# Attention and an MLP mixer on one core: next batch's work shared out by phase, low parts one product later, weight sums moved to VectorE

## The chip, the cores and the metric

The kernel runs on one core of a Trainium2 chip. The time is the device time of one execution in microseconds (us); lower is better. A core has five engines that each take their instructions from a queue in a fixed order: PE (TensorE, matmuls and transposes), DVE (VectorE), ACT (ScalarE), POOL (GpSimd) and SP (SyncE, which here starts DMA transfers). An engine whose next instruction waits for another engine holds everything that is queued behind it.

## The reference

There are B=8 batches, H=8 heads, S=576 positions and D=64 dims per head, all in f32. Attention comes first: a downsampled one (means over 4 positions, 144 x 144 scores) and a local one (each position sees those less than 4 away), added. Then a token MLP and a channel MLP with residuals.

```python
q_d, k_d, v_d = means of q, k, v over 4 positions
out_up = repeat(softmax(scale * q_d @ k_d.T) @ v_d, 4)
out_local = softmax(where(abs(i - j) < 4, scale * q @ k.T, -1e9)) @ v
x = (out_up + out_local) laid out as [B, S, H*D]          # 576 x 512
h = relu(x.T @ w_tok1) @ w_tok2                           # 512 x 576, hidden 256
u = x + h.T
out = u + relu(u @ w_ch1) @ w_ch2                         # hidden 1536
```

## The kernel before, in words

**Numbers.** A product of f32 matrices is emulated: each operand is scaled by a power of two and parted into a high and a low f16 part, and `mm3` (L122 to L124) issues three matmuls, high x high and the two mixed ones. High parts are mostly written by ACT, low parts mostly by DVE, by a subtraction of the high part from the source.

**Stages.** For each batch there is attention, then the token MLP (`mix`, L661), then the channel MLP. Attention consists of four pieces of downsampled attention (two heads each, `pooled`) and five tiles of 128 rows (the last has 64) of local attention (`local`). A local tile goes through a chain of engines: scores `sc` (PE, L600), exponentials into `P` (ACT, L614), division by their sums (DVE, L619), transposes `pT` (PE, L623), their copy `pt` (ACT, L627), the product with the values `av` (PE, L636), and its copy `x` (ACT, L641). `mix` then makes f16 parts `xh` (ACT L678, DVE L680), the first token product `t1`, its ReLU `hid` (ACT L716, DVE L718), the second token product `t2`, and its eviction `u` (ACT L729) with a maximum `umx` (DVE L731). Of these maxima `everywhere` (L645 to L659) makes one scale: a transpose `um_t` and a small matmul `um_b` on PE with reductions on DVE between them. Last, `mixtures` (L761) cuts the operands of the first channel product: it forms sums and differences of quarters of `u` on POOL (L771) and parts seven blocks a11, s1, s2, a12, s4, s3 and a22 (ACT L782, DVE L784).

**Channel MLP.** For batches 0 and 1 the first product c1 is plain (`first`, `first_up`): 12 blocks of 128 hidden channels in each of two chunks of positions (256 and 320 wide), evicted by ACT (L876) and DVE (L878). From batch 2 on it is `product7` (L881): seven half-size products take the place of eight, for each of six pairs p of hidden blocks. They run in three PSUM banks P, Q and R; ACT copies partial results out (`plain`, L903: x1, m5 and u2), DVE adds the next product (x1 += Q L937, u2 += R L941, m5 += P L945), and `leave` (L906) makes of the four results the parts of `h`: the high part with the ReLU on ACT (L908), and at once the low part on DVE (L909). Each product is six matmuls. The seven products need three sums of weight blocks for each pair, `t123`, loaded by DMA (L918). The second product c2 (`second`, `second_up`) has four blocks of output rows in two chunks, 36 matmuls each, and DVE adds the result to `u` (L1021), which SP stores.

**Weight sums.** `weight_sums` (L963) makes these sums once, for six pairs. For each pair DVE adds high and low parts of four weight blocks back to f32 (L973: a1, b1, a2 and b2, in a pool "tm" of 6 buffers), POOL takes four differences (L983, L984, L988 and L993), and `parts` cuts each: the high part by ACT (L979), the low part by POOL (L980). Three results go to DRAM over SP (L990, L991), with two staging tiles ts12 and ts3 for all pairs; the fourth overwrites a part of the weights themselves (`CW`), so it has to follow the plain product of batch 1 that still reads them.

**Order.** The first part of the program, batch 0 and the preparation of weights, is ordered by a driver with due times (`drive`). From batch 1 on the channel MLP of batch b is the spine: after each of its steps `tick(n)` (L1125) emits steps of the side work, which is attention and `mix` of batch b+1 and the loads of batch b+2, until the side work that is emitted (in us of PE time by its own costs) has reached SIDE x done / (FR x 24 x S), with SIDE=42 and FR=0.9, where `done` counts the ticks. A batch has 24 x S ticks in all, half of them in the first product and half in the second. `weight_sums` takes turns with this side work from the second chunk of c1 of batch 1 on (L1141). Tile's scheduler then puts all that is emitted into one fixed order for each engine.

Of the kernel before, what the change touches and what calls it, by code (L numbers as in the profile page):

```python
# [14 lines left out]
ALU = mybir.AluOpType  # L15
# [28 lines left out]
def tile_ups_attention_mixer(ctx, tc, qk, vw, vr, w1, w2, c1, c2, out):  # L44
# [105 lines left out]
    def step(engine, us, *needs, at=None, take="", give=""):  # L150
        return engine, us, needs, at, take.split(), give.split()
# [729 lines left out]
    def product7(st, steps):  # L881
# [23 lines left out]

        def leave(src, r, i, h):  # L906
            o = h[:, i, :, HS * r:HS * r + HS]
            nc.scalar.activation(o[:, 0], src, AF.Relu)  # L908
            nc.vector.scalar_tensor_tensor(o[:, 1], src, 0.0, o[:, 0], ALU.max, ALU.subtract)  # L909
# [5 lines left out]
        for p in range(NP):  # L915
# [14 lines left out]
            m5 = plain(R, "m5", "A")  # L930
            yield step("P", us, ("uh", b, "s2"))
# [9 lines left out]
            nc.vector.tensor_tensor(u2, u2, R[:, :HS], ALU.add)  # L941
            leave(u2, 0, 1, h)
# [3 lines left out]
            leave(m5, 1, 1, h)  # L946
            if p + 1 < NP:
                yield step("P", us)
                old, P = P, bank(Qtag, "P")
                product(P, "a11", weights(fa + 2, 0), True, False)  # L950
                x1 = plain(P, "x1", "A")
            else:
                old = P
            yield step("P", us, ("uh", b, "a22"))
            product(old, "a22", weights(fb, 0), False, True)
            leave(old[:, :HS], 1, 0, h)
            for f in (fa, fb):
                make(("h", b, 0, f), now[0])
# [4 lines left out]
    def weight_sums():  # L963

        for p in range(NF // 2):
            sums.append(dram.tile([128, 3, 2, 256], F16, name=f"sums{p}"))
        for p in range(NF // 2):
            fa, fb = C1.fin[2 * p], C1.fin[2 * p + 1]
            y = {}
            for n, f, o in (("a1", fa, 0), ("b1", fb, 0), ("a2", fa, 256), ("b2", fb, 256)):  # L970
                yield step("V", 0.42)
                y[n] = T([128, 256], F32, "tm", f"{n}_{p}")
                nc.vector.tensor_tensor(y[n], f[:, 0, o:o + 256], f[:, 1, o:o + 256], ALU.add)  # L973
            if p == 0:
                ts12 = T([128, 2, 2, 256], F16, "uh", "ts12")
                ts3 = T([128, 2, 256], F16, "uh", "ts3")

            def parts(src, o):
                nc.scalar.copy(o[:, 0], src)  # L979
                nc.gpsimd.tensor_sub(o[:, 1], src, o[:, 0])  # L980

            yield step("G", 2.0)
            nc.gpsimd.tensor_sub(y["a1"], y["b1"], y["a1"])  # L983
            nc.gpsimd.tensor_sub(y["b1"], y["b2"], y["b1"])  # L984
            parts(y["a1"], ts12[:, 0])
            parts(y["b1"], ts3)
            yield step("G", 2.0)
            nc.gpsimd.tensor_sub(y["b2"], y["b2"], y["a1"])  # L988
            parts(y["b2"], ts12[:, 1])
            nc.sync.dma_start(sums[p][:, 0:2], ts12)  # L990
            nc.sync.dma_start(sums[p][:, 2], ts3)  # L991
            yield step("G", 2.0, ("c1", 1, 1, 2 * p + 1))
            nc.gpsimd.tensor_sub(y["a2"], y["a2"], y["b2"])  # L993
            parts(y["a2"], fb[:, :, 0:256])
        make(("sums",), now[0])
# [121 lines left out]
    for b in range(1, B):  # L1117
# [24 lines left out]
        else:  # L1142
# [3 lines left out]
            while g.next is not None:  # L1146
                g.go()
                tick(2 * S / 7)
        banks = {}
        g, u = Run(second(st, banks)), Run(second_up(st, banks))  # L1150
        for c in range(4):
            for ch in range(2):
                for k in range(3):
                    g.go()
                    if k == 2:
                        u.go()
                    tick(CHUNKS[ch][1])
# [50 lines left out]
```

## Time and profile before

| what | us |
|---|---|
| median of 3 runs | 987.17 |
| lowest and highest | 985.52 and 989.9 |
| the profiled execution | 980.41 |
| its span in the trace | 978.6 |
| mean granted TensorE clock | 0.967 |

The profile is of one execution, which took 980.41 us; its trace spans 978.6 us of that, and the remaining 1.8 us lie around the span. In the views below, "busy" counts the time in which an engine carries out instructions. PEclk is the granted TensorE clock as a share of full speed. A row of the timeline gives start, duration, engine, line, operation, result<-operands, size and, in brackets, how long the engine stood idle ahead of it and what released it. L numbers are lines of the kernel before.

### The profile page before, as it was taken

To read this page: it belongs to the slowest core of one execution; us is meant where nothing else is said; L and a number is where in the kernel's file an instruction comes from. 1 tells how busy PE (TensorE), PEld (TensorE's weight loads), DVE (VectorE), ACT (ScalarE), POOL (GpSimd) and SP (SyncE) were. 2 spreads that over 40 slices of the span, in tenths; PEclk is the share of its full clock that TensorE was granted. 3 is DMA by queue.
4 is the path that set the end of the run, shared out by engine and by line. 5 is a ranking of instruction groups with operands and counts; after the bars stand their busy time and mean duration, and the time that the engine had idled before them with its cause. 6 is when DMAs were issued, how large, how long until landed. Compare 5 with 4: busy or idle time off the path is not lost.

```text
span 978.6 us, 26351 instructions
## 1 busy us (share of the span) xinstructions
PE 898.3 (92%) x11218; PEld 662.2 (68%) x11218; DVE 530.0 (54%) x1263; ACT 426.2 (44%) x1028; POOL 305.8 (31%) x457
## 2 busy tenths in 40 slices
PE   7887899998879988899989999899989999899998
PEld 3544678677656756677766767577666767677786
DVE  7797886336572275624663266723764256723631
ACT  4764673335451165613662154712654145612520
POOL 5899940424763021602034021422034020002000
PEclk9778999999799989999999999999999999999999
DMA  9693331510325113510136013520136011100111
GB/s 260 181 300 103 117 85 37 176 45 29 96 61 164 35 40 105 185 36 25 55 98 178 19 37 99 160 61 25 52 84 195 25 36 42 46 28 25 56 30 37
DMA packets 35142, 84.87 MB, mean 87 GB/s; under 512 B 4272, under 2 KB 15536, under 8 KB 33776
## 3 DMA queue, kind: packets, MB, share of 16 engines
q1 hardware_dynamic: 32464, 80.82, 27.0%
q10 hardware_dynamic: 2560, 2.36, 0.9%
q8 instruction: 88, 1.44, 0.6%
q14 instruction: 30, 0.25, 0.1%
HBM read 69.01 MB, written 11.80 MB: 83 GB/s over the span
## 4 chain that ended last, share of the span: by engine, by line
PE 64%; DVE 15%; ACT 8%; POOL 6%; issue 4%; DMA 4%; ACTq 0%; POOLq 0%; SPq 0%; DVEq 0%
PE c L124 31%; PE t L124 9%; PE P L124 7%; PE ad L567 3%; PE R L124 3%; DMA vw<-od 3%; PE t L702 2%; ACT pd L551 2%; DVE xh L680 2%; PE td L558 2%; PE Q L124 1%; DVE h L909 1%; PE busy L168 1%; PE av L636 1%; PE sc L600 1%
## 5 line engine op out<-in xcount | busy, mean ns | idle before, releaser
L124 PE MATMUL c<-h,CX 128*128 128x320 f16 (+1 forms) x2304 | 304.2, 287 | 0.0
L124 PEld LDWEIGHTS <-CX 128*128 128x128 f16 x2304 | 223.3, 98 | 64.3 <-issue 3.4
L124 PEld LDWEIGHTS <-CW 128*128 128x128 f16 x1440 | 137.4, 100 | 46.0 <-issue 7.2
L487 POOL TENSOR_TENSOR vr<-vr 72x256 f32<-72x256 f32 x64 | 48.7, 760 | 194.1 <-ACT dump L484 193.7
L1021 DVE SCALAR_TENSOR_TENSOR u<-c,io,u 128x256 f32<-128x256 f32 (+1 forms) x64 | 33.0, 515 | 125.4 <-PE c L124 124.8
L771 POOL TENSOR_TENSOR s<-u,u 128x288 f32<-128x288 f32 x12 | 9.3, 796 | 266.9 <-ACT u L729 266.9
L729 ACT ACTIVATE u<-t,down 128x256 f32<-128x256 f32 (+1 forms) x64 | 29.9, 498 | 139.3 <-PE t L124 139.3
L124 PE MATMUL c<-uh,CW 128*128 128x256 f16 (+1 forms) x576 | 82.6, 296 | 0.2 <-DVE h L878 0.2
L124 PEld LDWEIGHTS <-t 128*128 128x128 f16 x648 | 61.5, 99 | 23.8 <-issue 8.3
L731 DVE TENSOR_REDUCE umx<-u 128x1 f32<-128x256 f32 (+1 forms) x64 | 27.8, 451 | 86.0 <-ACT u L729 86.0
L124 PE MATMUL t<-xh,W 128*128 128x512 f16 (+1 forms) x240 | 60.5, 385 | 4.1 <-DVE xh L680 3.6
L513 POOL TENSOR_TENSOR qs<-qk 128x288 f32<-128x288 f32 x56 | 42.5, 759 | 69.3 <-DMA qk<-in_qk_dram 65.3
L124 PE MATMUL t<-W,hid 128*128 128x256 f16 (+1 forms) x384 | 58.5, 289 | 0.0
L680 DVE SCALAR_TENSOR_TENSOR xh<-x,back,xh 128x512 f16<-128x512 f32 (+1 forms) x40 | 35.4, 886 | 28.8 <-ACT xh L678 28.8
L567 PE MATMUL ad<-vd,ptd 72*72 72x65 f32 x512 | 41.4, 236 | 5.5 <-issue 3.3
L678 ACT ACTIVATE xh<-x,back 128x512 f16<-128x512 f32 (+1 forms) x40 | 29.0, 726 | 39.5 <-PE t L124 37.3
L567 PEld LDWEIGHTS ad<-vd,ptd 72*72 72x72 f32 x512 | 38.5, 151 | 10.7 <-issue 4.9
L551 ACT ACTIVATE pd<-sd,nmd 72x144 f32<-72x144 f32 x128 | 37.5, 374 | 16.7 <-DVE nmd L546 13.0
L623 PE MATMUL pT<-ident,P 128*128 128x128 f32 (+1 forms) x160 | 25.7, 286 | 19.4 <-DVE P L619 12.6
L484 ACT ACTIVATE dump<-vr 72x512 uint8<-72x512 f32 x64 | 39.9, 624 | 7.5 <-DMA vr<-in_vr_dram 7.2
L641 ACT ACTIVATE x<-av,up 128x512 f32<-128x512 f32 (+1 forms) x40 | 27.2, 679 | 36.8 <-PE av L636 36.7
L716 ACT ACTIVATE hid<-t 128x512 f16<-128x512 f32 x16 | 9.6, 597 | 73.7 <-PE t L124 65.6
(182 smaller groups left out, 1635.6 us busy)
## 6 DMA issues: line engine op xcount, KB each, us to landing
qk<-in_qk_dram SPq DMA_DIRECT2D x32, 579.0 KB
t<-sums SPq DMA_DIRECT2D x36, 384.0 KB
vw<-in_vw_dram SPq DMA_DIRECT2D x32, 351.0 KB
vr<-in_vr_dram SPq DMA_DIRECT2D x64, 144.0 KB
C_raw<-in_c_dram SPq DMA_DIRECT2D x16, 512.0 KB
out_dram<-u SPq DMA_DIRECT2D x32, 160.0 KB
C_raws<-in_c_dram SPq DMA_DIRECT2D x8, 512.0 KB
out_dram<-u SPq DMA_DIRECT2D x32, 128.0 KB
```

The costliest lines, as they stand in the source:

```text
L124: nc.tensor.matmul(ps, lhs(a), rhs(c), start=first and i == 0, stop=last and i == 2, **kw)
L484: nc.scalar.activation(dump, t.rearrange("p r c -> p (r c)"), AF.Square, scale=2.0 ** -20, accum_out=st.vm[:, i:i + 1])
L487: nc.gpsimd.tensor_add(t[:, 0:2], t[:, 0:2], t[:, 2:4])
L513: nc.gpsimd.tensor_add(two, x[:, :, 0:2], x[:, :, 2:4])
L551: nc.scalar.activation(pd[:, par, g], s[:, par, g], AF.Exp, bias=nm[:, par, g:g + 1], scale=0.125 / 16)
L567: nc.tensor.matmul(ps[:, g, par], pt[:, par, kg, G * g:G * g + G], st.vd[:, kg, 2 * pr + par], start=kg == 0, stop=kg == 1)
L641: nc.scalar.activation(x.rearrange("p hp two d -> p two hp d"), ps[:n, :, :4 * D].rearrange("p two (hp d) -> p two hp d", hp=4), AF.Copy, ...
L678: nc.scalar.activation(st.xh[t][:, 0], xf(t), AF.Copy, scale=back[:n])
L680: nc.vector.scalar_tensor_tensor(st.xh[t][:, 1], xf(t), back[:n], st.xh[t][:, 0], ALU.mult, ALU.subtract)
L729: nc.scalar.activation(st.u[c][:, s0:s0 + N], banks[ch, c // 2][:, c % 2, :N], AF.Copy, scale=st.down)
L731: nc.vector.tensor_reduce(st.umx[:, ch, c:c + 1], st.u[c][:, s0:s0 + N], axis=AX.X, op=ALU.max, apply_absolute_value=True)
L1021: nc.vector.scalar_tensor_tensor(u, banks[c, ch], io[:, ch:ch + 1], u, ALU.mult, ALU.add)
```

## The change

It has three parts.

1. **Shares by phase.** In the loop around `product7` a tick counts two thirds of what it did, and in the loop around `second` four thirds for batches from 2 on. The total stays 24 x S, with 8 x S in the first product and 16 x S in the second. Batch 1 is not altered.
2. **Low parts later.** `leave` issues the high part and puts the low part on a list; `rests()` empties the list behind the next product's own eviction or addition. `leave(m5)` now stands behind the next pair's a11 product.
3. **Weight sums.** All four differences of a pair are taken by DVE, high parts are copied by POOL (a new instruction form there) in place of ACT, and low parts stay on POOL. Each difference and each parting is a step of its own, and each pair has a gate: it may start only when a named product of batch 1 has been emitted. Lines are shifted: in the kernel after, the sums are L984, the differences L991, the copies L993 and the low parts L994; `leave` is L910 and the low part L916.

```diff
+        later = []
         def leave(src, r, i, h):
             o = h[:, i, :, HS * r:HS * r + HS]
             nc.scalar.activation(o[:, 0], src, AF.Relu)
-            nc.vector.scalar_tensor_tensor(o[:, 1], src, 0.0, o[:, 0], ALU.max, ALU.subtract)
+            later.append((src, o))
+        def rests():
+            while later:
+                src, o = later.pop(0)
+                nc.vector.scalar_tensor_tensor(o[:, 1], src, 0.0, o[:, 0], ALU.max, ALU.subtract)
...
             m5 = plain(R, "m5", "A")
+            rests()
...
             nc.vector.tensor_tensor(u2, u2, R[:, :HS], ALU.add)
+            rests()
             leave(u2, 0, 1, h)
...
             nc.vector.tensor_tensor(m5, m5, P[:, :HS], ALU.add)
-            leave(m5, 1, 1, h)
+            rests()
...
                 product(P, "a11", weights(fa + 2, 0), True, False)
                 x1 = plain(P, "x1", "A")
+            leave(m5, 1, 1, h)
             yield step("P", us, ("uh", b, "a22"))
             product(old, "a22", weights(fb, 0), False, True)
+            rests()
             leave(old[:, :HS], 1, 0, h)
...
     def weight_sums():
+        gates = [("c1", 1, 1, 3), ("c1", 1, 1, 7), ("c1", 1, 1, 11), ("c2", 1, 0, 0), ("c2", 1, 1, 0), ("c2", 1, 0, 1)]
...
-                yield step("V", 0.42)
+                yield step("V", 0.42, gates[p])
                 y[n] = T([128, 256], F32, "tm", f"{n}_{p}")
                 nc.vector.tensor_tensor(y[n], f[:, 0, o:o + 256], f[:, 1, o:o + 256], ALU.add)
...
-            def parts(src, o):
-                nc.scalar.copy(o[:, 0], src)
-                nc.gpsimd.tensor_sub(o[:, 1], src, o[:, 0])
-            yield step("G", 2.0)
-            nc.gpsimd.tensor_sub(y["a1"], y["b1"], y["a1"])
-            nc.gpsimd.tensor_sub(y["b1"], y["b2"], y["b1"])
-            parts(y["a1"], ts12[:, 0])
-            parts(y["b1"], ts3)
...
+            for x, z, o in (("b1", "a1", ts12[:, 0]), ("b2", "b1", ts3), ("b2", "a1", ts12[:, 1]), ("a2", "b2", fb[:, :, 0:256])):
+                yield step("V", 0.42)
+                to = {("b1", "a1"): "a1", ("b2", "b1"): "b1", ("b2", "a1"): "b2", ("a2", "b2"): "a2"}[x, z]
+                nc.vector.tensor_tensor(y[to], y[x], y[z], ALU.subtract)
+                yield step("G", 1.5)
+                nc.gpsimd.tensor_copy(o[:, 0], y[to])
+                nc.gpsimd.tensor_sub(o[:, 1], y[to], o[:, 0])
...
-                tick(2 * S / 7)
+                tick(2 * S / 7 * 2 / 3)
...
-                    tick(CHUNKS[ch][1])
+                    tick(CHUNKS[ch][1] * (4 / 3 if b > 1 else 1))
```

Three places show how instructions move. The first is POOL while the weights are prepared, in batch 0. L231 and L234 cut weights of the second channel product (`C2_raw`); `a1_0` to `b2_0` are sums of pair 0, `a1_1` and `b1_1` of pair 1. Before:

```order
L231 TENSOR_SCALAR C2_raw3_1123<-C2_raw3_1123 128x512
L984 TENSOR_TENSOR b1_0_3520<-b2_0_3550,b1_0_3520 128x256
L988 TENSOR_TENSOR b2_0_3550<-b2_0_3550,a1_0_3517 128x256
L234 TENSOR_SCALAR C2_raw2_1113<-C2_raw2_1113 128x512
L231 TENSOR_SCALAR C2_raws4_1129<-C2_raws4_1129 128x512
L993 TENSOR_TENSOR a2_0_3524<-a2_0_3524,b2_0_3550 128x256
L983 TENSOR_TENSOR a1_1_3605<-b1_1_3625,a1_1_3605 128x256
L234 TENSOR_SCALAR C2_raw3_1123<-C2_raw3_1123 128x512
```

After, the same stretch of POOL holds the weight cutting alone; the five differences that stood here and a little ahead of it are on DVE.

The second place is DVE in the first product of batch 1, second chunk. `h1_0` is the output of the blocks `c1_1_1_0` and `c1_1_1_1`, `a1_3` to `b2_3` belong to pair 3 of the weight sums, and `ad2_2`, `rd2_2` and `od2` to the third downsampled piece of batch 2. Before:

```order
L878 SCALAR_TENSOR_TENSOR h1_0_3109<-c1_1_1_0_3491,h1_0_3109 128x320
L973 TENSOR_TENSOR a1_3_3907<-CW6_151 128x256
L973 TENSOR_TENSOR b1_3_3930<-CW7_152 128x256
L878 SCALAR_TENSOR_TENSOR h1_0_3109<-c1_1_1_1_3535,h1_0_3109 128x320
L973 TENSOR_TENSOR a2_3_3933<-CW6_151 128x256
L573 TENSOR_SCALAR rd2_2_3573<-ad2_2_3564 72x4
L574 RECIPROCAL rd2_2_3573<-rd2_2_3573 72x4
L575 TENSOR_TENSOR od2_3327<-ad2_2_3564,rd2_2_3573 72x4x64
```

After:

```order
L878 SCALAR_TENSOR_TENSOR h1_0_3109<-c1_1_1_0_3491,h1_0_3109 128x320
L984 TENSOR_TENSOR a1_3_4210<-CW6_151 128x256
L984 TENSOR_TENSOR b1_3_4229<-CW7_152 128x256
L984 TENSOR_TENSOR b2_3_4245<-CW7_152 128x256
L991 TENSOR_TENSOR a1_3_4210<-b1_3_4229,a1_3_4210 128x256
L991 TENSOR_TENSOR b1_3_4229<-b2_3_4245,b1_3_4229 128x256
L878 SCALAR_TENSOR_TENSOR h1_0_3109<-c1_1_1_1_3529,h1_0_3109 128x320
L573 TENSOR_SCALAR rd2_2_3557<-ad2_2_3548 72x4
L991 TENSOR_TENSOR b2_3_4245<-b2_3_4245,a1_3_4210 128x256
L574 RECIPROCAL rd2_2_3557<-rd2_2_3557 72x4
L984 TENSOR_TENSOR a2_3_4248<-CW6_151 128x256
L575 TENSOR_TENSOR od2_3327<-ad2_2_3548,rd2_2_3557 72x4x64
```

Between the eviction of block 0 and `od2` there were three sums and now stand four sums and three differences; the gates set when a step is emitted, and the scheduler's order of the engine puts it earlier than that.

The third place is ACT near the end of `product7` of batch 3, while the side work of batch 4 runs beside it. `h3_4` and `h3_5` are outputs of pairs 4 and 5; `pT4_1`/`pt4_1` and `av4_1`/`x4_1` belong to the second local tile of batch 4, `vr5` to values of batch 5, `xh4_0` to the token MLP of batch 4. Before:

```order
L627 COPY pt4_1_7030<-pT4_1_7025 128x512
L484 ACTIVATE dump_128,vm5_7444<-vr5_5_7626 72x512
L614 ACTIVATE P2_112<-P2_112 128x8x38
L484 ACTIVATE dump_128,vm5_7444<-vr5_6_7678 72x512
L908 ACTIVATE h3_4_7015<-x13_3_6962 128x288
L641 ACTIVATE x4_1_7121<-av4_1_7050,up4_6264 128x2x4x64
L908 ACTIVATE h3_4_7015<-u23_4_7037 128x288
L627 COPY pt4_2_7107<-pT4_2_7102 128x512
L678 ACTIVATE xh4_0_7340<-x4_1_7121,back_129 128x512
```

After, these rows stand where pair 5 ends and c2 of batch 3 begins:

```order
L910 ACTIVATE h3_5_6998<-m53_5_7006 128x288
L484 ACTIVATE dump_128,vm5_7523<-vr5_7_7768 72x512
L910 ACTIVATE h3_5_6998<-P_3_4_6941 128x288
L627 COPY pt4_1_7153<-pT4_1_7148 128x512
L614 ACTIVATE P2_112<-P2_112 128x8x38
L641 ACTIVATE x4_1_7235<-av4_1_7177,up4_6278 128x2x4x64
L627 COPY pt4_2_7215<-pT4_2_7210 128x512
L678 ACTIVATE xh4_0_7420<-x4_1_7235,back_129 128x512
L627 COPY pt4_3_7243<-pT4_3_7238 128x512
```

The copies of local tiles 1 to 3 stood among evictions of `product7`, from pair 4 on; now they follow the last eviction of pair 5. On PE, 12 matmuls of c2 stand between `pT4_1` and `av4_1`, and 12 more between `pT4_2` and `pT4_3`. The last `t2` product of a batch stood 72 matmuls of c2 ahead of the next `product7` and now stands 48 ahead.

More of the change, by code (lines that the diff above doesn't have):

```diff
@@ L945, in product7 @@
             nc.vector.tensor_tensor(m5, m5, P[:, :HS], ALU.add)
-            leave(m5, 1, 1, h)
+            rests()
+            old = P
             if p + 1 < NP:
                 yield step("P", us)
-                old, P = P, bank(Qtag, "P")
+                P = bank(Qtag, "P")
                 product(P, "a11", weights(fa + 2, 0), True, False)
                 x1 = plain(P, "x1", "A")
-            else:
-                old = P
+            leave(m5, 1, 1, h)
             yield step("P", us, ("uh", b, "a22"))
             product(old, "a22", weights(fb, 0), False, True)
+            rests()
             leave(old[:, :HS], 1, 0, h)
-            for f in (fa, fb):
-                make(("h", b, 0, f), now[0])
+            if p + 1 == NP:
+                rests()
         make(("h", b), now[0])
@@ L969, in weight_sums @@
             y = {}
-            for n, f, o in (("a1", fa, 0), ("b1", fb, 0), ("a2", fa, 256), ("b2", fb, 256)):
-                yield step("V", 0.42)
+            for n, f, o in (("a1", fa, 0), ("b1", fb, 0), ("b2", fb, 256), ("a2", fa, 256)):
+                yield step("V", 0.42, gates[p])
                 y[n] = T([128, 256], F32, "tm", f"{n}_{p}")
@@ L976, in weight_sums @@
                 ts3 = T([128, 2, 256], F16, "uh", "ts3")
-            def parts(src, o):
-                nc.scalar.copy(o[:, 0], src)
-                nc.gpsimd.tensor_sub(o[:, 1], src, o[:, 0])
-            yield step("G", 2.0)
-            nc.gpsimd.tensor_sub(y["a1"], y["b1"], y["a1"])
-            nc.gpsimd.tensor_sub(y["b1"], y["b2"], y["b1"])
-            parts(y["a1"], ts12[:, 0])
-            parts(y["b1"], ts3)
[L987 to L994, printed above, removed]
+            for x, z, o in (("b1", "a1", ts12[:, 0]), ("b2", "b1", ts3), ("b2", "a1", ts12[:, 1]), ("a2", "b2", fb[:, :, 0:256])):
[5 more added lines that the diff above has]
+                nc.gpsimd.tensor_sub(o[:, 1], y[to], o[:, 0])
+                if o is ts3:
+                    nc.sync.dma_start(sums[p][:, 2], ts3)
+                if to == "b2":
+                    nc.sync.dma_start(sums[p][:, 0:2], ts12)
         make(("sums",), now[0])
```

## The prediction

> **What bounds the kernel now.** I read the busy time by engine first.
>
> ```profile
> PE 898.3 (92%) x11218; PEld 662.2 (68%) x11218; DVE 530.0 (54%) x1263; ACT 426.2 (44%) x1028; POOL 305.8 (31%) x457
> ```
>
> PE is busy for 898.3 of 978.6 us. The change takes no work from PE, so all that it can win is in the 80.3 us in which PE stands idle, and in the time in which PE runs at a lower granted clock. Where these lie is shown by busy time in windows that I cut at the stage bounds. Columns: window, length, busy us (x instructions) of PE, PEld, DVE, ACT and POOL, then PEclk, DMA share and GB/s. The rows are c1 and c2 of batch 1, then `product7` and c2 by turns for batches 2 to 6, then `product7` of batch 7.
>
> ```profile
> 215.50:286.90 71.40, 59.32 (x824) 45.13 (x822) 43.90 (x104) 37.15 (x104) 42.85 (x64) 0.90 0.18 56
> 286.90:348.00 61.10, 58.96 (x614) 42.88 (x613) 19.78 (x47) 14.73 (x32) 18.87 (x34) 0.97 0.33 103
> 348.00:408.60 60.60, 52.95 (x952) 39.61 (x952) 43.49 (x106) 40.24 (x103) 14.29 (x23) 0.94 0.32 100
> 408.60:460.40 51.80, 51.80 (x394) 38.42 (x393) 14.29 (x39) 8.71 (x19) 13.39 (x24) 1.00 0.18 54
> 460.40:520.80 60.40, 52.87 (x980) 39.74 (x979) 43.65 (x107) 39.92 (x105) 14.30 (x23) 1.00 0.33 103
> 520.80:572.50 51.70, 51.70 (x393) 38.32 (x391) 14.20 (x38) 8.61 (x19) 13.29 (x24) 1.00 0.20 54
> 572.50:634.30 61.80, 54.10 (x984) 40.03 (x982) 44.99 (x108) 40.06 (x106) 14.96 (x25) 1.00 0.34 107
> 634.30:687.30 53.00, 51.55 (x395) 38.28 (x394) 15.33 (x39) 10.38 (x23) 13.89 (x23) 1.00 0.16 46
> 687.30:745.40 58.10, 53.33 (x969) 40.24 (x970) 41.31 (x104) 37.83 (x100) 12.42 (x21) 0.97 0.35 106
> 797.10:856.10 59.00, 52.98 (x980) 39.83 (x978) 42.03 (x106) 35.39 (x89) 1.51 (x2) 1.00 0.15 45
> 907.20:940.50 33.30, 32.17 (x261) 25.15 (x259) 18.99 (x46) 16.77 (x41) 0.00 (x0) 1.00 0.18 54
> ```
>
> Two kinds of stage lose time. The five `product7` stages with side work leave PE idle for 7.65, 7.53, 7.70, 4.77 and 6.02 us, 33.67 in sum, while the c2 stages between them leave at most 1.45, with DVE busy for 14 us of 52 and ACT for 9. The last `product7`, without side work, loses 1.13. And c1 of batch 1, in which the weight sums are made, leaves 12.08 us idle at a mean clock of 0.90.
>
> What PE waits for in one `product7` stage (460.4 to 520.8) is told by PE's waits. Columns: line, releaser, total us, count, longest.
>
> ```profile
> PE pT L623 <- DVE P L619: 2.5, 4, 1.2
> PE P L124 <- ACT x L903: 1.4, 2, 0.8
> PE av L636 <- DMA vw<-od: 1.0, 1, 1.0
> PE sc L600 <- ACT x L641: 0.8, 1, 0.8
> PE td L558 <- ACT pd L551: 0.6, 1, 0.6
> PE P L124 <- DVE x L937: 0.5, 1, 0.5
> ```
>
> The chains of attention own 2.5 + 0.8 + 0.6, the first products (P <- x) own 1.4 + 0.5, and one transfer owns 1.0: 6.8 of 7.53 us; smaller waits share the remaining 0.7.
>
> **The shares by phase.** Two thirds of the tick means that PE's order has about two products between pieces of attention where it had one and a half. A product lasts 32.17 / 42 = 0.77 us in the stage without side work, so a chain step gets 1.53 us of cover for 1.15. The longest wait on a chain step is 1.2 us, beyond the cover of 1.15; with 0.38 us more, waits under that size go and the larger ones shrink. What remains of the local tiles moves into c2, where by the order 12 matmuls stand between one step and the next.
>
> ```profile
> 457.19 3.43 PE L124 MATMUL c<-h,CX 128*128 128x320 f16 x24
> ```
>
> That is 1.72 us for 12, by the row of 24 matmuls of c2, and c2 has DVE and ACT nearly free. So of a stage's 7.53 us I let the attention waits go (7.53 less 1.9 for the first products and 1.0 for the transfer, which the change doesn't touch): -4.6. Taken back: c2 holds some chain waits that it didn't have, and only 12 matmuls in place of 24 stand between the last `t1` and the first `t2` while ACT and DVE make `hid`. I put 0.8 on that, between 0 (all covered by 1.72 us a step) and 2.5 (the four transposes wait as now).
>
> The scale of the mixtures comes out of `um_t` and `um_b`, and what then comes first in `product7` is the block a11. These are its rows on PE and on ACT.
>
> ```profile
> 457.94 0.96 ACT L782 ACTIVATE a11h<-u,us 128x288 f16<-128x288 f32 x2 [6.15 <-DVE us L130]
> 460.46 0.90 PE L124 MATMUL P<-a11h,CW 128*128 128x288 f16 x6
> 464.33 0.90 PE L124 MATMUL P<-s2h,t 128*128 128x288 f16 x6 [0.85 <-ACT x L903]
> ```
>
> ACT stood idle for 6.15 us until the scale came, and parted a11 at 457.94; PE had c2 matmuls to do until 460.46, so 1.6 us were to spare behind ACT's part. In the order, the last `t2` now stands 48 matmuls ahead of P instead of 72: 24 matmuls, 3.43 us, less. The distance from `um_b` to P shrinks only from 24 to 20 matmuls, 0.57 us of the 1.6. It still holds, but the mixtures on POOL and the parts on ACT start that much later, and `product7` takes up one block after another: I take +0.5 a batch (0 to 3.4, if all the lead was needed). Per batch this is -4.6 + 0.8 + 0.5 = -3.3, and for five batches **-16.5**, between about -30 (all idle time but the start's last microsecond goes) and +3.
>
> Batch 1's c2 isn't re-shared, but the order has the last `t2` of batch 2 behind its last matmul, where 12 matmuls followed before: **+1.7**, the cover that is gone.
>
> **Low parts later.** As many instructions as before. DVE's additions into x1, u2 and m5, on which a bank's release hangs, no longer queue behind a low part. P <- x L937 (0.5) may go; as more of `h`'s low parts end later, the last of them could meet c2's first matmuls, but c2 starts with pair 0. Counted at nothing, within -0.5 and +0.5 a batch.
>
> **Weight sums at the start.** In batch 0 five differences leave POOL, by the timeline:
>
> ```profile
> 72.81 1.17 POOL L983 TENSOR_TENSOR a<-b,a 128x256 f32<-128x256 f32 x1 [0.36 <-DVE b L973]
> 81.47 0.86 POOL L984 TENSOR_TENSOR b<-b,b 128x256 f32<-128x256 f32 x1
> 82.41 1.64 POOL L988 TENSOR_TENSOR b<-b,a 128x256 f32<-128x256 f32 x1
> 86.80 0.72 POOL L993 TENSOR_TENSOR a<-a,b 128x256 f32<-128x256 f32 x1
> 87.48 0.73 POOL L983 TENSOR_TENSOR a<-b,a 128x256 f32<-128x256 f32 x1
> 85.50 0.69 DVE L239 SCALAR_TENSOR_TENSOR CX<-C_raw 128x512 uint32<-128x512 uint32 x1 [1.25 <-POOL C_raw L234]
> ```
>
> They take 1.17 + 0.86 + 1.64 + 0.72 + 0.73 = 5.12 us of POOL, which cuts `C_raw` there while DVE waits for it (1.25 in the last row). DVE takes them into such waits. From 5.12 not all is on the path: **-2**, between 0 and -5.
>
> **Weight sums in c1 of batch 1.** This is what happens there now (timeline, then groups with count and busy, mean or shortest/mean/longest ns, and the windows around the stall):
>
> ```profile
> 251.52 0.88 DVE L973 TENSOR_TENSOR b<-CW 128x256 f32<-128x256 f16 x1 [1.93 <-POOL CW L980]
> 254.37 1.09 PE L623 MATMUL pT<-ident,P 128*128 128x128 f32 x4 [3.84 <-DVE od L575]
> 286.46 0.63 PE L623 MATMUL pT<-ident,P 128*128 128x128 f32 x4 [2.91 <-ACT ts L979]
> L973 DVE TENSOR_TENSOR a<-CW x12: 407/710/1296, 67.5 to 279.0; 128x256 f32<-128x256 f16 x12
> L980 POOL TENSOR_TENSOR ts<-b,ts x12: 661/672/903, 227.3 to 288.6; 128x256 f16<-128x256 f32 x12
> L979 ACT CAST ts<-b x12: 388/405/421, 225.1 to 286.0; 128x256 f16<-128x256 f32 x12
> L231 POOL TENSOR_SCALAR C_raw<-C_raw x16: 650/797/1690, 38.9 to 79.8; 128x512 uint32<-128x512 uint32 x16
> 222.00:225.50 3.50, 1.00 (x14) 0.52 (x10) 2.40 (x7) 3.08 (x10) 2.15 (x4) 1.00 0.01 2
> 225.50:230.00 4.50, 4.50 (x29) 3.44 (x30) 2.95 (x12) 2.64 (x9) 3.88 (x7) 0.62 0.17 62
> 254.40:264.00 9.60, 9.60 (x77) 6.53 (x78) 5.25 (x10) 3.53 (x10) 8.90 (x15) 0.51 0.20 72
> ```
>
> A sum on DVE waits for a buffer of "tm" that POOL still reads, `od` queues behind the sum, and PE waits for `od`: 3.84 us idle, and then 9.60 us at a clock of 0.51, which costs 9.60 x 0.49 = 4.7 more. One such jam is worth 8.5 us. The Trainium skill ("TensorE: Matmul & The Clock Gate", Part 1) says that the clock halves after an idle window of about 3.4 us and returns after about as long a busy one. By it a jam would cost 3.84 + 1.7 = 5.5; the row of 9.60 us at full busy time and 0.51 speaks against so quick a return, and 0.62 in the 4.50 us behind a window with 2.50 us of idle time against so long an onset, so I keep 4.7.
>
> What the change does: 24 casts leave ACT (24 x 0.405 = 9.7 us). 19 differences leave POOL, at 0.72 to 0.86 each 14 to 16 us, and come to DVE (19 x 0.41 to 0.71 = 8 to 13 us). 24 high parts come to POOL; a copy there isn't in the trace, so it lies between 0.33 (half of the shortest L231, which has twice the elements) and 0.67 (L980, of the same size with one operand more). I take 0.5, nearer to the row of one operand: 12 us, with 8 to 16 as ends. So POOL has 39 to 41 us, DVE 52 to 57, ACT 27: none reaches 71.4. It is a matter of order. DVE's queue now holds every sum and difference, and each sum waits for a buffer that POOL must release: what is queued behind is `od`, the eviction of c1's blocks (L878) and, behind these, PE. By the order `od2_2` stands behind 4 sums and 3 differences where it stood behind 3 sums, so I keep the jam of 8.5 at that place, and let the wait for `ts` on ACT (2.91) go, as that instruction no longer exists. Against it I set 1.9, one wait of DVE for POOL (the 1.93 above) that passes to PE: **-1**, between -12 (idle time and half clock go) and +17 (two jams more).
>
> **The sum.** -16.5 + 1.7 - 2 - 1 = -17.8. From the profiled 980.41 us that gives 962.6; the median of the runs shown is 6.8 above the profiled one, so from 987.17 the forecast is 969.4, **969**. From 982.2 to 992.1, within 0.5% of the median, is about what a measurement of this kernel can tell from no change.
>
> **Rivals.**
>
> *The waits move along.* The waits of the local tiles might sit in the chain and not in the cover: then c2 stalls for what `product7` no longer does. For: pT waits for DVE P in both cases by order. Against: DVE and ACT are busy for a quarter and less of c2. Time: the term of -4.6 a batch falls away with its 0.8, leaving +0.5 x 5 + 1.7 - 2 - 1 = +1.2: 988. No change.
>
> *DVE jams on POOL, slower.* In c1 of batch 1 each sum may stall DVE, and PE behind it, for long enough to halve the clock, at 8.5 us a jam. For: POOL was the releaser of DVE's waits (1.93), and all buffers now pass through DVE, POOL and DVE again. Against: POOL's sum of work falls. It ends above 992.1 if 23 us more are lost, that is with three more jams: -17.8 + 25.5 = +7.7, 995.
>
> *Nearly all idle time goes.* -30 in `product7`, the jam and its half clock gone (-8.5) with the 2.91, and -3 at the start, +1.7: -42.7, 944. For: chains with 1.53 us of cover against waits of at most 1.2. Against: the first products' waits are not touched.
>
> *Both at once are slower on SBUF.* DVE's sum and POOL's subtraction ran side by side around 251.5 and the sum took 0.88 where the shortest took 0.41. If all 19 differences and 18 sums in the stage take 0.47 more, DVE has 17 us more, about 70 of 71.4, and becomes the bound there; half of the 17 would land on PE: 969 + 8.5 = 978. The Trainium skill ("GPSIMD Engine Reference", Specifications) says that GpSimd shares its SBUF interfaces with VectorE and contends with instructions of two SBUF inputs, which these are; the longest sum of 1296 ns agrees.
>
> **How the numbers follow.** The forecast has 0.57 (its own range 957 to 979), the waits that move 0.14, the jams 0.09, the larger gain 0.12, the contention 0.08. Faster by over 0.5%: 0.57 + 0.12 + 0.08 = 0.77; within: 0.14; slower: 0.09. The range reaches down to 947, which leaves out some of the larger gain, and up to 988, which leaves out the jams.
>
> **What would show it.** Right: `product7` stages with side work under 57 us with less than 4 us of idle PE, c2 stages longer by the work moved and with under 2 us idle; c1 of batch 1 within 71 +/- 5 us, a stall before `pT` of batch 2 behind `od`; POOL copies of about 0.5 us. Wrong: idle time in c2 as large as what left `product7`; PE waiting for `um_b` or a11 at the start of `product7`; a clock near 0.5 for more than 10 us of c1 of batch 1.

## The result, and the profile after

| | us |
|---|---|
| after, median of 4 runs | 962.63 (962.29 to 963.37) |
| before, median of 4 runs beside them | 986.35 (983.91 to 989.9) |
| ratio, 95% interval | 0.9758 (0.9726 to 0.9789) |
| the profiled execution of after, its span | 963.37, 961.6 |

The change makes the kernel 23.7 us faster by medians; 969 was forecast, in a range of 947 to 988. The two profiled executions differ by less: 978.6 - 961.6 = 17.0 us of span. Both differences are taken up below. Two executions in the experiments, one of 1728.49 us and one of 1257.29 us, lie far outside the other runs of their kernels and are left out of every figure.

The windows of the kernel after, cut at its own stage bounds, have the same columns as before: c1 and c2 of batch 1, `product7` and c2 for batches 2 to 6, then the last `product7`.

```profile
214.90:286.70 71.80, 59.87 (x889) 46.05 (x887) 52.30 (x126) 32.38 (x86) 44.63 (x74) 0.90 0.20 62
286.70:347.00 60.30, 56.66 (x553) 41.55 (x549) 17.83 (x45) 12.50 (x27) 14.87 (x27) 0.99 0.32 97
347.00:398.40 51.40, 47.87 (x682) 36.10 (x682) 36.08 (x88) 33.24 (x87) 9.57 (x14) 0.91 0.25 73
398.40:455.90 57.50, 57.42 (x665) 42.21 (x664) 21.24 (x56) 16.16 (x32) 18.01 (x32) 1.00 0.30 89
455.90:506.30 50.40, 46.36 (x708) 35.73 (x706) 35.99 (x90) 33.49 (x91) 9.53 (x14) 1.00 0.27 78
506.30:564.00 57.70, 57.49 (x664) 42.13 (x663) 21.15 (x56) 16.09 (x32) 17.92 (x32) 1.00 0.31 88
564.00:614.60 50.60, 46.66 (x711) 36.04 (x710) 36.34 (x90) 33.77 (x92) 9.74 (x15) 1.00 0.27 80
614.60:675.20 60.60, 58.33 (x671) 42.31 (x669) 23.55 (x59) 17.75 (x37) 19.12 (x33) 1.00 0.30 82
675.20:725.30 50.10, 45.95 (x698) 35.32 (x699) 33.96 (x87) 31.51 (x88) 7.67 (x13) 1.00 0.27 79
725.30:782.80 57.50, 57.42 (x665) 42.20 (x663) 21.31 (x55) 15.99 (x32) 17.88 (x33) 1.00 0.31 88
782.80:832.00 49.20, 46.19 (x707) 35.70 (x706) 35.07 (x90) 29.27 (x77) 1.97 (x2) 1.00 0.20 59
832.00:889.60 57.60, 57.19 (x661) 41.88 (x660) 21.96 (x50) 17.67 (x35) 6.01 (x8) 1.00 0.06 20
889.60:923.40 33.80, 32.03 (x259) 25.05 (x258) 21.61 (x51) 18.59 (x46) 0.51 (x1) 1.00 0.18 53
```

Read it row against row. `product7` of batch 3 was 60.40 us with 7.53 idle and is 50.40 with 4.04; the c2 behind it was 51.70, full, and is 57.70 with 0.21 idle. So 10 us left the one and 6 came to the other: work moved, and about 3.5 us of waiting didn't move with it. The five `product7` stages have 3.53, 4.04, 3.94, 4.15 and 3.01 us of idle PE, 18.67 in sum where there were 33.67. DVE in these c2 stages goes from 14 to 16 us to 21 to 24 and is still far from full.

PE's waits in `product7` of batch 3 (455.9 to 506.3) are now these, all that the view lists. Columns: line, releaser, total us, count, longest.

```profile
PE P L124 <- DVE m L954: 1.7, 1, 1.7
PE P L124 <- ACT x L903: 0.8, 1, 0.8
PE td L558 <- ACT pd L551: 0.8, 1, 0.8
PE Q L124 <- DVE h L916: 0.7, 1, 0.7
```

The four waits of `pT` for DVE (2.5), that of `sc` (0.8) and that of the transfer (1.0) are gone from this stage; the products wait for their own evictions (m, x, h) more than before, 3.2 us where they waited 2.1.

In c1 of batch 1 the timeline of PE has both old stalls again, the second a little later, and no wait for ACT's casts at the end:

```profile
227.51 0.28 PE L652 MATMUL vm_t<-ident,vm_m 72*1 72x72 f32 x1 [4.84 <-DVE vm_m L649]
257.00 0.99 PE L623 MATMUL pT<-ident,P 128*128 128x128 f32 x4 [3.93 <-DVE od L575]
342.74 0.27 PE L652 MATMUL um_t<-ident,um_m 128*1 128x128 f32 x1 [0.65 <-DVE um_m L649]
344.90 0.38 PE L658 MATMUL um_b<-um_m,ones 1*128 1x1 f32 x2 [1.90 <-DVE um_m L655]
347.00 0.40 PE L124 MATMUL P<-a11h,CW 128*128 128x288 f16 x1 [1.10 <-ACT a11h L782]
```

The last three rows are the end of c2 of batch 1, where the order had put the last `t2` behind all matmuls of c2: 0.65 + 1.90 + 1.10 = 3.65 us, with nothing to cover them. The stage is 60.30 long nevertheless, 0.8 less than before.

### The profile page after: what moved, and what is told of

Same layout as the page of the kernel before. It is cut to its first block, busy times and chain, and to the rows that moved or that the text cites. A ratio compares the mean times of both kernels' runs of the same rounds, so it can differ in the third digit from the quotient of the medians.

```text
span 961.6 us, 26341 instructions
## 1 busy us (share of the span) xinstructions
PE 892.8 (93%) x11218; PEld 660.7 (69%) x11218; DVE 538.3 (56%) x1287; ACT 424.7 (44%) x1004; POOL 300.2 (31%) x457
## 4 chain that ended last, share of the span: by engine, by line
PE 73%; DVE 16%; ACT 5%; issue 3%; DMA 1%; POOL 1%; ACTq 0%; POOLq 0%; DVEq 0%; SPq 0%
PE c L124 32%; PE t L124 10%; PE P L124 9%; PE R L124 4%; PE av L636 3%; PE ad L567 3%; PE sc L600 2%; PE t L702 2%; PE Q L124 2%; PE busy L168 2%; PE pT L623 2%; PE td L558 2%; PE sd L539 1%; DVE CX L239 1%; DVE uh L757 1%
## 5 line engine op out<-in xcount | busy, mean ns | idle before, releaser
L124 PE MATMUL c<-h,CX 128*128 128x320 f16 (+1 forms) x2304 | 310.0, 286 | 3.0 <-DVE u L949 2.0
L487 POOL TENSOR_TENSOR vr<-vr 72x256 f32<-72x256 f32 x64 | 52.6, 821 | 196.2 <-ACT dump L484 189.5
L513 POOL TENSOR_TENSOR qs<-qk 128x288 f32<-128x288 f32 x56 | 39.3, 701 | 94.5 <-DMA qk<-in_qk_dram 90.9
L680 DVE SCALAR_TENSOR_TENSOR xh<-x,back,xh 128x512 f16<-128x512 f32 (+1 forms) x40 | 33.0, 825 | 57.3 <-ACT xh L678 56.2
L124 PEld LDWEIGHTS <-hid 128*128 128x128 f16 x384 | 34.9, 99 | 11.1 <-ACT hid L716 1.8
L636 PE MATMUL av<-vw,pt 47*32 47x64 f32 x2304 | 36.5, 234 | 5.4 <-DMA vw<-od 3.4
```

The costliest lines, as they stand in the source:

```text
L124: nc.tensor.matmul(ps, lhs(a), rhs(c), start=first and i == 0, stop=last and i == 2, **kw)
L487: nc.gpsimd.tensor_add(t[:, 0:2], t[:, 0:2], t[:, 2:4])
L513: nc.gpsimd.tensor_add(two, x[:, :, 0:2], x[:, :, 2:4])
L636: nc.tensor.matmul(ps[QB * j:QB * j + QB, par, D * hp:D * hp + D], pt[p, hp, QB * j:QB * j + QB], st.vw[h][p, g, D * hp:D * hp + D], start ...
L680: nc.vector.scalar_tensor_tensor(st.xh[t][:, 1], xf(t), back[:n], st.xh[t][:, 0], ALU.mult, ALU.subtract)
```

## The experiments

Times are ratios to the kernel before, run beside it on the same chip. Kernels are compared by stages as well, because one part varies from execution to execution: the start. The kernel before was run unchanged for a second profile.

> The kernel before, unchanged, for a second profile. All theories: ratio 1.0 within the spread of 0.6%. If this execution is slower than the 980.4 of the first profile, the stage in which it is longer tells what varies: by theory C c1 of batch 1 (the clock after the stall); otherwise the start, or the product7 stages alike.

Its median was 985.76 against 985.2, ratio 1.0012 (0.999 to 1.0034). Its windows are the start (to c1 of batch 1), c1 and c2 of batch 1, and the five pairs of `product7` and c2 as one:

```profile
0.00:220.60 220.60, 191.85 (x2425) 133.30 (x2432) 153.27 (x344) 115.49 (x250) 126.07 (x171) 0.90 0.47 143
220.60:352.80 132.20, 114.47 (x1437) 85.58 (x1435) 64.14 (x152) 51.54 (x136) 61.73 (x96) 0.97 0.26 78
352.80:913.00 560.20, 524.10 (x6813) 390.73 (x6813) 289.01 (x714) 241.74 (x601) 118.11 (x190) 0.99 0.24 71
```

The same windows of the first profile of before:

```profile
0.00:215.50 215.50, 189.01 (x2431) 130.78 (x2432) 153.26 (x344) 115.22 (x250) 126.22 (x171) 0.91 0.49 147
215.50:348.00 132.50, 118.28 (x1436) 88.01 (x1434) 63.68 (x151) 51.88 (x136) 61.72 (x96) 0.94 0.25 78
348.00:907.20 559.20, 524.07 (x6813) 390.69 (x6813) 289.38 (x714) 241.90 (x601) 117.86 (x190) 0.99 0.24 71
```

The start took 5.1 us longer, the two other windows 0.7 in sum. So in this pair of profiles the variation isn't in c1 of batch 1, where theory C put it. Over the thirteen profiles that are read here the start lies between 214.6 and 220.6. So medians that differ by 5 us can differ by starts; stage sums tell parts of the change apart better.

**One part at a time.** The edits are the three parts of the diff, each put into the kernel before alone. This is the one for the shares; the two others are as in the section on the change.

```diff
-                tick(2 * S / 7)
+                tick(2 * S / 7 * 2 / 3)
...
-                    tick(CHUNKS[ch][1])
+                    tick(CHUNKS[ch][1] * (4 / 3 if b > 1 else 1))
```

> Before with only the new tick shares (two thirds in product7, four thirds in c2 from batch 2). Theory A, the gain is the spreading of attention and mix over c2: 15 to 18 us faster than before, ratio 0.982 to 0.985, the five product7 stages with side work near 50 us with 3 to 4 us of idle PE, the c2 stages near 57.5. Theory B, the later low parts free the banks of product7 and are the gain: within 5 us of before. Theory C, the weight sums are the gain: within 5 us of before.

Measured 0.985 (0.983 to 0.9871), 970.73 us. Its stages are read from a second run of the same kernel:

> Before with the new shares only, a second time, for a profile of it. If the shares alone give what the first comparison said: 0.983 to 0.987, and the five pairs of product7 and c2 at 545 to 548 us together, against 559 before and 538 to 543 after, with more idle PE in c2 of batches 2 to 4 than the kernel after has (theory D: low parts made at once hold back the evictions there). If the first figure was off: 0.978 to 0.982 and pairs at 540.

Measured 0.9833 (0.9806 to 0.9859), 969.47 us; both figures stand. The five pairs as one window:

```profile
349.20:894.80 545.60, 522.85 (x6814) 391.58 (x6814) 287.88 (x709) 245.73 (x597) 116.84 (x190) 0.99 0.25 73
```

The pairs fell by 13.6 us from 559.2, and PE's idle time in them from 35.1 to 22.8. That is most of the gain, and not all: with the whole change the pairs take 540 or so. The low parts alone (`later` and `rests`, and `leave(m5)` behind a11):

> Before with only the later low parts. Theory A: within 3 us of before, ratio 0.997 to 1.003; PE's waits for DVE x and ACT x in product7 change by less than 0.5 us a batch. Theory B: 10 us or more faster, ratio under 0.99. Theory C: within 3 us.

Measured 1.0008 (0.9991 to 1.0025): nothing. The pairs take 560.60 us.

The weight sums alone (the new `weight_sums` with DVE's differences, POOL's copies and the gates):

> Before with only the new weight sums. Theory A: 0 to 4 us faster, ratio 0.996 to 1.0; the stall ahead of od in c1 of batch 1 stays at 3 to 4 us. Theory B: the same. Theory C, the sums make the part of the gain by medians (23.7 us) that the two profiled executions (17 us) don't show, because the old sums are sometimes slower than in the profiled execution: 6 to 8 us faster by medians, ratio 0.992 to 0.994, and the runs lie as close together as those of the kernel after (1 us) where those of before spread over 6.

Measured 0.997 (0.9956 to 0.9984), 3.1 us, with runs from 980.26 to 986.33: as wide as before, so theory C falls here too. c1 and c2 of batch 1, then the pairs:

```profile
218.30:348.10 129.80, 116.34 (x1436) 87.30 (x1434) 70.90 (x170) 44.79 (x113) 59.48 (x101) 0.94 0.25 79
348.10:908.40 560.30, 524.13 (x6813) 390.65 (x6813) 290.67 (x714) 242.06 (x600) 116.97 (x190) 0.99 0.24 71
```

The three ratios add to 0.983, 17 us, and the whole change had given 0.976. Something in the parts helps something else.

**Two parts at a time**, beside the kernel after.

> The kernel after, unchanged, timed beside the next three on one chip. It was 0.9758 of the kernel before; the parts alone gave 0.985 (shares), 0.997 (sums) and 1.0008 (low parts), which add to 0.983. If the parts simply add and the first comparison was high by the spread of before: 0.981 to 0.984. If they help each other: 0.974 to 0.978.

Measured 0.9742 (0.9712 to 0.9771), 962.12 us. It is not the spread: the parts help each other.

> The kernel after without the later low parts. Adding: 0.982, the same as the kernel after. Theory D, with the local tiles out of product7 its chain of products and evictions is what PE waits for there, and later low parts shorten this only then: 4 to 6 us slower than the kernel after, 0.980 to 0.982 where that is at 0.976, with waits of PE in product7 for ACT x or DVE x of 1.5 to 2.5 us a stage where the kernel after has 1.

Measured 0.9785 (0.9756 to 0.9814), 965.67 us, 3.6 us slower than after.

> The kernel after with the old weight sums. Adding: 0.985 to 0.986. Theory D: 0.978 to 0.980, as it lacks only the 3 us of the sums. Theory E, the sums are worth more with the new shares since what they move in c1 of batch 1 also frees the start of the next stages: 0.983 to 0.986, with c1 and c2 of batch 1 together 5 us or more longer than in the kernel after.

Measured 0.979 (0.976 to 0.982), 965.71 us, also 3.6 us slower. c1 and c2 of batch 1 are 132.40 us, against 132.10 and 130.80 in the two profiles of after: 1.6 longer at most, not the 5 of theory E.

> The kernel after with the old shares. All theories: 0.996 to 0.999, since sums gave 3 us alone and low parts nothing; if it is under 0.992, sums and low parts help each other without the shares and the gain by shares is smaller than thought.

Measured 0.9956 (0.9935 to 0.9977), 982.64 us. The two without the shares stay near what the sums give alone.

The pairs of these kernels, first of shares with sums and without later low parts:

```profile
349.00:894.80 545.80, 522.57 (x6814) 390.55 (x6814) 288.84 (x709) 245.91 (x596) 116.55 (x190) 0.99 0.25 73
```

Shares with later low parts and the old sums:

```profile
348.70:888.90 540.20, 519.82 (x6814) 389.18 (x6814) 286.21 (x709) 244.93 (x597) 117.78 (x190) 0.99 0.25 74
```

The kernel after, second profile:

```profile
345.40:883.50 538.10, 518.07 (x6814) 388.74 (x6814) 286.52 (x709) 245.38 (x596) 117.33 (x190) 1.00 0.25 74
```

So the later low parts take the pairs from 545.6 to 540.2 with the old sums, 5.4 us, and from 545.8 to 542.6 or 538.1 with the new ones, by the two profiles of after: 3.2 or 7.7 us, with 3.6 by medians. Where the shares are old they are worth nothing (560.6 alone; 560.10 with the sums, whose own is 560.3). Theory D forecast 4 to 6, which fits the mean. Of its mechanism one place is shown: among PE's waits from `product7` of batch 2 on, that of the first c2 matmuls for an addition on DVE is halved. First shares and sums without later low parts, then the second profile of the kernel after:

```profile
PE c L124 <- DVE u L941: 3.9, 2, 1.9
PE c L124 <- DVE u L949: 2.0, 2, 1.0
```

The other waits of the product chain that theory D named (for x on ACT) do not shrink. From 23.2 us the idle time falls to 20.0, by 3.2; the other 4.5 us are PE's busy time for the same 6814 matmuls. The granted clock accounts for most of that: summed over its records in the pairs, the time lost to a lower clock (length x missing share) is 6.1 us in the first and 2.2 in the second. c2 of batch 2 shows it, in the same two profiles and order; PE is busy throughout in both:

```profile
399.70:458.40 58.70, 58.62 (x664) 42.93 (x663) 20.73 (x55) 15.68 (x30) 16.95 (x30) 0.98 0.29 84
395.20:452.60 57.40, 57.32 (x664) 42.14 (x662) 21.12 (x55) 16.12 (x32) 17.79 (x32) 1.00 0.29 88
```

58.62 x 0.98 = 57.4. The lower clock lies right behind the hand-over from `product7` to c2: 0.50 from 399.7 to 402.2 in the first of the two, and 0.50 from 400.6 to 404.0 in the kernel with the shares alone, behind waits of 1.92 and 1.93 us. In the five profiles that have the new shares (two thirds and four thirds) and the later low parts, the two of after among them, the clock is 1.00 in the 4 us behind that hand-over. So the shorter wait there comes with a clock that stays up, in all seven.

**The stall in c1 of batch 1.** Sums of pairs 2 to 5 are held back by data: each buffer first takes one element that the last block of c1 produced.

```diff
                 y[n] = T([128, 256], F32, "tm", f"{n}_{p}")
+                if p > 1:
+                    nc.vector.tensor_copy(y[n][:, 0:1], ready[1].h7[NF // 2 - 1][:, 1, 1, S - 1:S])
...
-                if ch == 0:
+                if ch == 1:
                     work.g = together([weight_sums(), work.g], 2)
```

> The kernel after, with sums of pairs 2 to 5 made behind the last block of c1 of batch 1: each sum's buffer first takes one element of that block's output. Theory F, the sums' queue on DVE is what stalls PE in c1 of batch 1 (4.8 and 3.9 us in the kernel after, and half clock behind them): c1 falls from 70.5 to 72 us to 60 to 64, c2 of batch 1 grows from 60.3 by 0 to 3, in sum 6 to 10 us faster than the kernel after, ratio to before 0.965 to 0.969. Rival G, the stall belongs to the chain of attention (ad, rd, od) that is in c1 anyway: c1 stays above 68, and the ratio is 0.974 to 0.978.

Measured 0.978 (0.9756 to 0.9805), 962.92 us: no gain over the kernel after. c1, then c2 of batch 1:

```profile
218.00:281.70 63.70, 55.91 (x920) 43.55 (x917) 36.98 (x94) 33.50 (x88) 25.98 (x43) 0.97 0.17 50
281.70:347.60 65.90, 58.33 (x528) 41.87 (x517) 36.62 (x94) 11.12 (x26) 33.84 (x58) 0.97 0.33 108
```

Theory F holds for the length of c1, 63.70 us, and for one of the two stalls: that before `pT` behind `od` is gone, and the clock is 0.97. But 5.6 us came back in c2, which the theory put at 0 to 3. Where, PE's waits in c2 of that kernel (with the start of `product7`) show:

```profile
PE pT L623 <- DVE P L619: 1.9, 1, 1.9
PE um_b L658 <- DVE um_m L655: 1.9, 1, 1.9
PE t L124 <- DVE hid L718: 1.7, 2, 1.3
PE P L124 <- ACT a11h L782: 1.1, 1, 1.1
PE um_t L652 <- DVE um_m L649: 0.7, 1, 0.7
```

Of 7.3 us, 3.7 are the uncovered end of the stage, which the kernel after has too (3.65), and 3.6 are steps of attention and of the token MLP that wait for DVE, which now has the sums too (36.62 us busy where 17.83 were). The end of the stage led to the last kernel. The other stall of c1 stayed, so it isn't the work of pairs 2 to 5:

```profile
230.51 0.28 PE L652 MATMUL vm_t<-ident,vm_m 72*1 72x72 f32 x1 [4.79 <-DVE vm_m L649]
```

In the kernel after, the rest of pair 1 stands on DVE right ahead of `vm_m` (227.31), 1.95 us where the kernel before had none of it:

```profile
224.26 0.67 DVE L984 TENSOR_TENSOR b<-CW 128x256 f32<-128x256 f16 x1
225.19 0.61 DVE L984 TENSOR_TENSOR a<-CW 128x256 f32<-128x256 f16 x1
225.72 0.67 DVE L991 TENSOR_TENSOR b<-b,b 128x256 f32<-128x256 f32 x1
```

The stall grew by 2.34 us. That these three make most of it is argued from the order; no run moves them alone.

**More to c2.**

```diff
-                tick(2 * S / 7 * 2 / 3)
+                tick(2 * S / 7 / 2)
...
-                    tick(CHUNKS[ch][1] * (4 / 3 if b > 1 else 1))
+                    tick(CHUNKS[ch][1] * (3 / 2 if b > 1 else 1))
```

> The kernel after with a half and three halves in place of two thirds and four thirds, so that still more side work goes to c2. Theory A, what is left of idle PE in product7 (3 to 4 us a stage) is still side work: product7 44 to 46 us a stage, c2 62, pairs 3 to 8 us shorter in sum, ratio to before 0.967 to 0.972. Rival H, what is left belongs to the products' own chain (P <- m, Q <- h) and to the start of product7, where the scale of the mixtures comes later: the pairs stay within 2 us or get longer, ratio 0.974 to 0.980.

Measured 0.9786 (0.9761 to 0.9812), 965.27 us. The pairs are 543.1 us, against 538.1 to 542.6 in the kernel after: the time that rival H forecast. `product7` and c2 of batch 2:

```profile
347.20:391.40 44.20, 42.34 (x438) 33.16 (x438) 30.31 (x75) 28.84 (x75) 5.64 (x9) 0.95 0.21 64
391.40:453.90 62.50, 61.39 (x908) 44.61 (x907) 25.00 (x64) 19.52 (x41) 21.93 (x36) 1.00 0.33 97
```

`product7` falls by 5.6 us from the 49.80 of the second profile of after and idles 1.86, but c2 grows by 5.1 from 57.40 and idles 1.11 where it was full. So rival H's reason isn't what is seen in this batch: of the 4.03 us that `product7` idled there, over half went with the side work. In the pairs PE idles 18.9 us, less than the 20.0 and 21.7 of the kernel after, but is busy for 524.2 where that is for 518.1 and 520.9, and the last batch takes 73.9 us where others with the new shares take 71.9 or 72.0. More side work in c2 gains nothing more.

**The end of c2 of batch 1.** The last kernel has the sums in c2 and lets batch 1's side work go ahead in c2 like that of the others.

```diff
-                    tick(CHUNKS[ch][1] * (4 / 3 if b > 1 else 1))
+                    tick(CHUNKS[ch][1] * (4 / 3 if b > 1 else 4 / 3))
```

> The kernel with sums of pairs 2 to 5 in c2 of batch 1, and batch 1's c2 ticks at four thirds as well, so that the last t2 of batch 2 stands 72 matmuls of c2 ahead of product7 and not behind all of them. If the cover behind the last t2 is what the end of that stage lacks (PE waits there of 0.65, 1.89 and 1.09 us in the kernel with the sums in c2): these go, c2 of batch 1 falls from 65.9 to 61 to 63 us, c1 stays at 63 to 65, the rest within 1 us a stage, ratio 0.972 to 0.975. If the denser side work meets the sums on DVE and loses it again: c2 stays at 65 or more, ratio 0.977 to 0.980.

Measured 0.971 (0.9684 to 0.9736), 958.18 us, the fastest of all; the kernel with the sums in c2 had 0.978. c1 and c2 of batch 1, and `product7` of batch 2:

```profile
219.10:283.80 64.70, 56.53 (x920) 43.87 (x917) 37.44 (x94) 33.62 (x88) 25.77 (x43) 0.95 0.16 49
283.80:346.60 62.80, 56.90 (x512) 40.66 (x500) 38.14 (x98) 14.22 (x31) 35.72 (x60) 0.97 0.33 105
346.60:395.10 48.50, 45.43 (x699) 35.48 (x700) 33.19 (x82) 30.34 (x83) 7.61 (x13) 1.00 0.30 90
```

c2 fell by 3.1 to 62.80 and `product7` of batch 2 by 3.1 from 51.6, c1 grew by 1.0. The waits of `um_t` (0.65), `um_b` (1.89) and a11 (1.09) at the end of the stage are gone: 30 matmuls of c2 now stand behind `um_b`. In their place PE waits 1.54 us for the parting of a22 ahead of `product7`, and in c2 the `t` products wait 2.1 for the copies on DVE that hold the sums back (0.7 and 1.4). The cover was what the end of that stage lacked.

## Why the prediction was right

By stages the change is summed here. Each entry is a mean over the profiles that share that part: for the start, and for c1 and c2 of batch 1, five with the old sums and eight (start) or six (c1 and c2, where no sums are held back) with the new ones; for the pairs, five with the old shares, two with the new shares alone or with sums, and four with the later low parts too.

| part | forecast | measured by stages |
|---|---|---|
| shares by phase, five pairs | -16.5 | 560.1 to 545.7: -14.4 |
| low parts, with the new shares | 0 (within 2.5) | 545.7 to 540.5: -5.2 |
| sums, c1 and c2 of batch 1, cover included | -1 + 1.7 = +0.7 | 132.2 to 130.5: -1.7 |
| sums at the start | -2 | 217.9 to 217.5: -0.4, spread 6 |
| last batch | 0 | 71.5 to 71.9: +0.4 |
| sum | -17.8 | -21.3 |

The sum is closer than its terms, and that is luck in part: against the forecast the shares fell 2.1 us short, the start 1.6 and the last batch 0.4, while the low parts brought 5.2 more and the weight sums 2.4.

**The main term held, by its mechanism.** Waits of attention's chains went out of `product7` and c2 covered them. With the shares alone PE's idle time in the pairs falls from 35.1 to 22.8 us, which is 12.4 of the 13.6 us that the pairs lose there. In the kernel after, with the low parts, the forecast was off both ways: 33.67 - 18.67 = 15.0 us of idle PE left `product7`, 3.0 a batch where 4.6 was said, and c2 took back 0.3 a batch (idle PE there, five batches: 0.08 + 0.21 + 2.27 + 0.08 + 0.41 = 3.05 against 1.45) where 0.8 was said. At the start of `product7`, put at +0.5, PE waits for an operand only in batch 2 (1.10 us for a11, behind 1.90 before `um_b`), which was a sign of being wrong in the prediction's own list. Of its signs of being right, the two limits on idle time are just missed: 4.04 and 4.15 us in two of the `product7` stages where under 4 was said, and 2.27 in one c2 where under 2 was. The rival in which the waits move along is out: full c2 stages took 6 us of work with 0.2 of idle time. So is the one in which nearly all idle time goes, as 18.67 us stayed, and the jams did not multiply: c1 of batch 1 has two long stalls as it had.

**The step that was mis-sized is the low parts, "counted at nothing, within -0.5 and +0.5 a batch".** They measure about -1.0 a batch, though only with the new shares. The forecast priced them in the profile of before, where PE had other waits in `product7`. Once those were gone, PE waited 1.92 us at the hand-over from `product7` to c2 of batch 2 for an addition on DVE, and ran at a clock of 0.50 behind it; with later low parts it waits 1.02, and the clock stays at 1.00. A term of nothing should have been priced against the profile that the other parts leave.

**The weight sums came out 2.4 us better, from errors that partly cancel.** The jam at `od` stayed, as forecast (3.93 us), and the wait for ACT's casts went. A second stall grew, from 2.50 to 4.84 us, in front of `vm_t`, for which the forecast has no term. The forecast also kept 4.7 us of lost clock behind `od`, taken from one execution. These are windows of the kernel after, two behind the first stall and one behind the second:

```profile
227.50:232.00 4.50, 4.49 (x21) 3.10 (x22) 3.65 (x15) 2.64 (x9) 2.08 (x4) 0.50 0.17 62
232.00:237.00 5.00, 5.00 (x56) 4.71 (x54) 1.73 (x6) 2.04 (x4) 1.07 (x2) 0.88 0.00 0
257.00:262.00 5.00, 5.00 (x60) 3.97 (x65) 2.99 (x7) 1.25 (x4) 4.60 (x10) 0.66 0.22 80
```

They cost 4.50 x 0.50 + 5.00 x 0.12 = 2.9 and 5.00 x 0.34 = 1.7. In the second profile of before the stall of 3.83 us at the same place was followed by 4.60 us at 0.63, which is 1.7 too, so the 4.7 belongs to one execution and isn't a fixed price of the jam. By the Trainium skill ("TensorE: Matmul & The Clock Gate", Part 1) about 3.4 us at half rate would cost 1.7 by estimate. The prediction had set that size aside for the 9.60 us of the profile before; the traces show it and larger ones. The gain of the sums isn't the clock's: over c1 and c2 of batch 1 PEclk is 0.94 to 0.97 in the five profiles with the old sums and 0.94 or 0.95 in the six with the new ones. It is idle time of PE, 16.2 us in the mean with the old sums and 14.1 with the new.

By engine, c1 of batch 1 has DVE at 52.30 us (52 to 57 forecast), POOL at 44.63 (39 to 41 forecast) and ACT at 32.38 (27 forecast); more of the side work stands there than before, with 889 instructions on PE where there were 824. POOL's copy took 0.39 to 0.66 us, with 0.5 forecast:

```profile
L993 POOL CAST ts<-b x12: 393/582/661, 221.1 to 274.1; 128x256 f16<-128x256 f32 x12
```

The cover that is gone at the end of c2 of batch 1 cost more than the 1.7 forecast: the waits are 3.65 us in the kernel after, and giving the cover back, in the kernel with the sums in c2, saved 3.1 in that stage. The rival of contention is out at its size: it needs DVE busy for about 70 us of c1, and DVE has 52.30, and 53.61 in the second profile of after. Single sums do take longer in some executions: the group of b has a median of 0.66 us in the first profile of after and 0.87 in the second, where the kernel before had 0.58.

**The start** gained nothing that its own spread lets through. Of the forecast -2, POOL's relief in the first 215 us is visible (126.22 us busy before, 122.75 and 121.74 in the two profiles of after), the path's isn't.

By medians the change is worth 23.7 and 25.0 us in two comparisons, where the stages give 21. The starts of the kernel after were the shortest of all in both its profiles (214.9 and 214.6), and 217.5 in the mean over kernels with the same start; whether that is chance or belongs to the whole kernel stays open. The profiled execution of before had a short start too (215.5), so the two spans, with starts alike, differ by only 17.0 us.

## What to carry to other kernels

Where side work shares a stage with a chain of dependent products, look for the stage in which the other engines are idle and give it the side work until the cover is used up: here two thirds and four thirds gained 14 us, and a half and three halves gained nothing more. Price each edit against the profile that the other edits leave, since a wait that is hidden now is next in line. When work is moved to a stage's end, look at what has to be computed behind it before the next stage can begin, and leave that some matmuls as cover.

## What the runs showed of the hardware that was not expected

- The start of this program differs by 5.1 us between two executions of the same instructions (215.5 and 220.6 us in the kernel before), while the 560 us of the five pairs repeat within 1.4 us over five profiles with the old shares.
- What a stall of 3.8 to 4.8 us costs afterwards in clock varies, even behind the same stall of the same kernel: 9.60 us at 0.51 in the first profile of before, 4.60 at 0.63 in the second. In the kernel after it was 4.50 at 0.50 with 5.00 at 0.88 behind it, and 5.00 at 0.66.
- Half clock can follow without any idle stretch of that length: in the kernel with shares and sums PE was busy for 1.54 of the 2.70 us up to 399.7, its longest wait was 1.92, and the next 2.50 us ran at 0.50.
- A copy from f32 to f16 of 128x256 took POOL 0.39 us at best and 0.58 in the median of one group, where ACT took 0.41 for the same.
